# Moving the second stage of batch 1 ahead of the first stage of batch 2 in a woven FFT and expert kernel

## The chip, the cores and the metric

The kernel runs on one core of one Trainium2 chip. The metric is the device time of one execution in microseconds (us). The time before is 1304.29 us, the median of three runs (1298.82 to 1309.32).

## The reference, cut to what matters

```
X = fft(x, axis=1); X = fft(X, axis=2); x = X.real      # 8 batches of 2496 x 256
logits = x @ w_gate                                     # 19968 rows, 8 experts
expert_idx = argmax(logits); gate_w = softmax(logits)[expert_idx]
for e in range(8):                                      # rows sorted by expert
    h = maximum(x_sorted[lo:hi] @ w1[e], 0)             # 256 -> 1024
    y_sorted[lo:hi] = h @ w2[e]                         # 1024 -> 256
out = gate_w * y                                        # in the old order of the rows
```

So each batch is first transformed (a Fourier transform over 2496 places, then one over 256 columns), each of its rows picks one of eight experts, and the rows go through that expert's two matrices.

## The kernel before, in words

The kernel treats the batches one after another and weaves three kinds of work into one order of instructions, written out by Python generators. Every engine then runs its own queue strictly in that order.

**First stage** (`first`, lines 325 to 347). A batch is loaded in three parts (`xq`, line 289, by SP's DMA queue). DVE folds each part (`fold`, lines 295 to 306), TensorE multiplies it by waves (tile `s`), ACT copies the result to `t` (line 321), and a DMA writes it to the scratch `Td` in DRAM (line 342; for batches above 1 it is issued by SP). After the third part `regroup` (line 354) reads `Td` back in another arrangement, as two tiles `t`.

**Second stage** (`second`, lines 361 to 413). For each half of a batch there is a small rotation (tile `pr`), then groups (TensorE `p<-table,t`, ACT copy `zz`, line 379), then five windows: TensorE `p<-table,zz`, ACT `zs` (line 405), DVE `lg` and `rows` (lines 408 and 410). The half ends in `route` (lines 416 to 457): DVE makes the one-hot choice `oh`, TensorE ranks the rows (`rk`), DVE works out the places. The half's ten sets of 128 rows then stand in the list `waiting`. `send` takes one of them, casts its places on ACT (`pi`, line 467) and scatters the rows to the table `Xs` with an indirect DMA of POOL (line 236). Batch 0's casts are not needed.

**Experts** (`experts`, lines 699 to 844). `plan` (lines 476 to 521) works out on DVE, on one partition, which expert and which rows each block of a round has. A block of 256, 128 or 512 rows is fetched from `Xs` by five DMAs of SP (`xb`, lines 532 and 536), with two more for its expert's weights (`w_sb`, lines 542 and 544). DVE and ACT turn the rows (`xT`, lines 580 and 583). TensorE multiplies by the first matrix (`ph`), ACT and DVE apply the relu in turn (`hT`, lines 796 and 794), TensorE multiplies by the second (`py`), ACT scales (`y`, line 835), and POOL scatters the rows to the output. The first round has two blocks of 256 rows and four of 128 from batch 0 alone, the second has blocks of 256 from batch 1.

**The order.** `mixed(b)` says what lies beside the experts: it weaves the first stage of batch b+1 with the second stage of batch b. The main loop takes a unit of expert work and then as many side steps as are due, with a `send` after each (batches under 4). Before the first block can be multiplied, the rows of batch 0 must be in `Xs` and fetched again. In the meantime TensorE has only side work. The fixed number of side steps before the first block is turned is 9 in line 744.

**The end.** `pads` scatters eight sets of padding rows to `Xs` (line 236), one after each of the first eight steps of the last round.

PSUM tiles of the side work share one tag with three buffers, `xq` has three buffers, weights have three.

Of the kernel before, what the change touches and what calls it, by code (L numbers as in the profile page):

```python
# [15 lines left out]
ALU = mybir.AluOpType  # L16
ACTF = mybir.ActivationFunctionType
AX_X = mybir.AxisListType.X
# [17 lines left out]
E, F = 8, 1024  # L36
# [10 lines left out]
def free(ap, offset, *dims):  # L47
    return bass.AP(ap.tensor, ap.offset + offset, [list(ap.ap[0])] + [list(d) for d in dims])


def bc(ap, axis, n):
    shape = list(ap.shape)
    shape.insert(axis, n)
    return ap[tuple([slice(None)] * axis + [None])].to_broadcast(shape)
# [129 lines left out]
LATE = 4  # L184
SHARE, EARLY, ROOM = 0.8, 0.7, 1.2
AHEAD = 12
WARM = 16
MOST = max(k for now in rounds() for _, k, _ in now)

# [26 lines left out]
def kernel(ctx: ExitStack, tc, x, w_gate, w1, w2, out):  # L216
    nc = tc.nc
    vec, act, pool = nc.vector, nc.scalar, nc.gpsimd

    def mm(o, lhsT, rhs, start=True, stop=True, **kw):  # L220
        nc.tensor.matmul(o, lhsT=lhsT, rhs=rhs, start=start, stop=stop, **kw)  # L221
# [47 lines left out]
    con, k = {}, 0  # L269
# [91 lines left out]
    def second(b):  # L361

        t4 = None

        def turn_last(h):

            nonlocal t4
            t4 = ahead.pop((b, "t4", h))
            n = min(HALF, NG - h * HALF)
            pr = pm_.tile([GP, HALF], F32, tag="m", name="pr")  # L370
            mm(pr[:, 0:n], con["rot"][:], t4[0:GP, 0:n, H])
            act.copy(t4[0:GP, 0:n, H], pr[:, 0:n])

        def group(g):
            i, n = g % HALF, LAST if g == NG - 1 else GP
            p2 = pm_.tile([128, 2, n], F32, tag="m", name="p2")
            for c in range(2):
                mm(p2[:, c], t4[0:GP, i, c * H:(c + 1) * H], con["m2"][:, c, 0:n])
            act.copy(zz[:, :, g * GP:g * GP + n], p2[:])  # L379
            if g == HALF - 1:  # L380
                turn_last(1)

        def mirror(rows, k):
            act.copy(free(rows[:], (k + 1) * W + D - 1, [-W, 2], [-1, H - 1]),
                     free(rows[:], k * W + 1, [W, 2], [1, H - 1]))

        turn_last(0)
        yield
        group(0)
        yield  # L390
        group(1)
        yield
        for h in range(2):
            rows = sp.tile([128, NSL, W], F32, tag="rows", name="rows")
            lg = sp.tile([128, NSL, E], F32, tag="lg", name="lg")
            for i in range(HW):
                w, k = HW * h + i, 2 * i
                if w + 2 < NG:
                    group(w + 2)
                p3 = pm_.tile([128, 2 * NY + 2 * E + 1], F32, tag="m", name="p3")  # L400
                z = zz[:, :, 128 * w:128 * (w + 1)]
                mm(p3[:, 0:NY + 2 * E], z[:, 0], con["rd"][:, 0, 0:NY + 2 * E], True, False, skip_group_check=True)
                mm(p3[:, NY:], z[:, 1], con["rd"][:, 1], False, True, skip_group_check=True)
                zs = sp.tile([128, NY + 1], F32, tag="zs", name="zs")
                act.copy(zs[:], p3[:, NY + 2 * E:])  # L405
                if i:
                    mirror(rows, k - 2)
                vec.tensor_copy(lg[:, k:k + 2], p3[:, NY:NY + 2 * E].rearrange("p (m e) -> p m e", m=2))  # L408
                for m, op in enumerate((ALU.add, ALU.subtract)):
                    vec.scalar_tensor_tensor(rows[:, k + m, 0:NY], p3[:, 0:NY], zs[:, 0:1], zs[:, 1:],  # L410
                                             op0=ALU.add, op1=op)
                yield
            mirror(rows, k)
            yield from route(b, h, rows, lg)
# [58 lines left out]
    bk = {n: bt[:, lo:hi] for n, (lo, hi) in where.items()}  # L473
    gone = bk["cap"]

    def plan(b, size, k, last):

        nonlocal gone

        def one(name, *dims, dt=F32):  # L480
            return cp.tile([1, *dims], dt, tag="p_" + name, name="p_" + name, bufs=2)

        nb, ni = one("nb", E), one("ni", E, dt=I32)
        ce, ex, rb, n = one("ce", E), one("ex", E), one("rb", E), one("n", E)
        lo = one("lo", E, E)
        vec.tensor_tensor(nb[:], base[0:1], gone[:], op=ALU.subtract)
        vec.tensor_scalar(ni[:], nb[:], size - 1.0 if last else 0.0, None, op0=ALU.add)
        vec.tensor_scalar(ni[:], ni[:], size.bit_length() - 1, None, op0=ALU.logical_shift_right)
        vec.tensor_copy(nb[:], ni[:])
        vec.tensor_tensor(lo[:], bk["low"].rearrange("p (a b) -> p a b", a=E), bc(nb[:], 1, E), op=ALU.mult)  # L490
        vec.reduce_sum(ce[:], lo[:], axis=AX_X)
        vec.tensor_tensor(ex[:], ce[:], nb[:], op=ALU.subtract)
        yield
        vec.scalar_tensor_tensor(rb[:], ex[:], -float(size), gone[:], op0=ALU.mult, op1=ALU.add)
        ge, ei = one("ge", MOST, E), one("ei", MOST)
        val, eq, rw = one("val", MOST, E + 1), one("eq", MOST, E + 1), one("rw", MOST)
        vec.tensor_tensor(ge[:], bc(bk["i"], 2, E), bc(ce[:], 1, MOST), op=ALU.is_ge)
        vec.reduce_sum(ei[:], ge[:], axis=AX_X)
        yield
        vec.tensor_tensor(eq[:], bc(ei[:], 2, E + 1), bc(bk["e9"], 1, MOST), op=ALU.is_equal)  # L500
        vec.memset(val[:, :, E:E + 1], float(E * CAP))
        vec.scalar_tensor_tensor(val[:, :, 0:E], bc(bk["i"], 2, E), float(size), bc(rb[:], 1, MOST),
                                 op0=ALU.mult, op1=ALU.add)
        yield
        vec.tensor_tensor(val[:], val[:], eq[:], op=ALU.mult)
        vec.reduce_sum(rw[:], val[:], axis=AX_X)
        tab = cp.tile([1, 2, MOST], I32, tag="p_tab", name="p_tab", bufs=4)
        vec.tensor_copy(tab[:, 0], rw[:])
        vec.tensor_scalar(tab[:, 1], ei[:], E - 1.0, None, op0=ALU.min)
        if last:  # L510
            cnt = cp.tile([1, 1], I32, name="cnt")
            vec.tensor_copy(cnt[:], ce[:, E - 1:E])
            tabs["cnt"] = cnt
        if not last:

            vec.tensor_scalar(n[:], ex[:], -1.0, float(k), op0=ALU.mult, op1=ALU.add)
            vec.scalar_tensor_tensor(n[:], n[:], 0.0, nb[:], op0=ALU.max, op1=ALU.min)
            nxt = one("gone", E)
            vec.scalar_tensor_tensor(nxt[:], n[:], float(size), gone[:], op0=ALU.mult, op1=ALU.add)
            gone = nxt  # L520
        yield
        tabs[b, size, last] = tab
# [68 lines left out]
    def below(w, eng):  # L591

        ws2 = sp.tile([128, 3, FC // 2, H], F32, tag="t4", name="ws2")
        return right(ws2, *(w[:, 4 * f:4 * f + 4, k * H:(k + 1) * H] for f in (1, 0) for k in range(2)), eng=eng)
# [104 lines left out]
    def experts(todo):  # L699
# [4 lines left out]
        xbs, got, xT, used, left, rest = [], [], None, None, None, None  # L704
# [30 lines left out]
        for k, (b, size, last, at) in enumerate(todo):  # L735
            n, m = size // 128, BIG // size
            if not k:
                while todo[0][:3] not in tabs:
                    yield 0, False
                fetch_some(0, 1)  # L740
                while b not in whole:
                    yield 0, True
                fetch_some(0)
                for _ in range(9):
                    yield 0, False
                for xT in turn(b, size, xbs[0][0]):
                    pass
# [53 lines left out]
            if follow:  # L801
# [9 lines left out]
                if follow[1] == BIG and quartered(*follow[:2]):  # L811
                    rest = below(got[0][1], pool)
# [30 lines left out]
            if follow and follow[1] == BLK and quartered(*follow[:2]):  # L843
                rest = below(got[0][1], vec)
# [29 lines left out]
    def ahead_of(b):  # L874

        yield from first(b)
        regroup(b, 0)
        regroup(b, 1)

    def mixed(b):  # L880

        one, two = (ahead_of(b + 1) if b + 1 < B else iter(())), second(b)
        for _ in range(3):
            next(one, None)
            yield
        for k, _ in enumerate(two):
            if k % 2:
                next(one, None)
            yield
        yield from woven(close(b), one)  # L890
        yield from through(b)
# [9 lines left out]
    nc.sync.dma_start(out=wg[:], in_=w_gate)  # L901
    for k in range(WARM):
        pw = pse.tile([128, D], F32, tag="bd"[k % 2], name="py")
# [35 lines left out]
    work = experts(todo)  # L939
    steps = {b: mixed(b) for b in range(1, B)}  # L940
    for b in range(1, B):

        done, due, room = 0, 0.0, 0.0
        side = chain(steps[b], islice(steps.get(b + 1, iter(())), AHEAD))
        ticks = TICKS + AHEAD * (b == 1)
        if b == 1:
# [23 lines left out]
        for _ in side:  # L970
            send()
    rest = pads(B - 1)
    for _ in work:
        next(rest, None)


_INS = ["x", "moe_w_gate", "moe_w1", "moe_w2"]
# [46 lines left out]
```

## Time and profile before

| what | value |
|---|---|
| median of three runs | 1304.29 us (1298.82 to 1309.32) |
| profiled execution, its own time | 1306.36 us |
| its span | 1304.6 us |
| mean granted TensorE clock | 0.970 |
| TensorE busy | 1227.3 us, 94% of the span |
| DVE, ACT, POOL busy | 54%, 33%, 28% |
| DMA | 249.71 MB, mean 191 GB/s |

The profile's second part cuts the span into 40 slices of 32.6 us and gives each engine's busy share in tenths. TensorE is at nine or more nearly everywhere except in the first eight slices. The chain that ended last is 86% TensorE. So what an edit is worth is what it takes from, or adds to, the time in which TensorE stands still.

### The profile page before, as it was taken

Reading aid. Unit: us, or ns where it says so; the run is one execution under the profiler, and the core shown is the slowest. Engines: PE = TensorE matmul, PEld = TensorE weight load, DVE = VectorE, ACT = ScalarE, POOL = GpSimd, SP = SyncE. Lnnn points to the kernel's source line nnn. Section 1 sums busy time; section 2 is a strip of 40 time slices with the busy share of each in tenths; the row PEclk is TensorE's granted clock in tenths of the full one; section 3 lists DMA queues with packets and bytes.
Section 4 is the critical chain, followed back from the end, with each engine's and each line's share of the span. In section 5 each row is a group of like instructions: output and inputs, shape, how many; then the busy total and the mean of one; then the engine's idle time right before and its main releaser. Section 6 shows DMA issues by size and latency. Waiting matters only on the chain.

```text
span 1304.6 us, 21062 instructions
## 1 busy us (share of the span) xinstructions
PE 1227.3 (94%) x6905; PEld 1080.0 (83%) x6905; DVE 700.7 (54%) x1772; ACT 436.0 (33%) x1096; POOL 361.8 (28%) x355
## 2 busy tenths in 40 slices
PE   5668898999999999999999999999999999999996
PEld 3557797876788888888888888888889999999995
DVE  4455433433456555566546455675468774444662
ACT  1423222332334343434334343432233332222232
POOL 0245215125014311351114411351354221111112
PEclk8869898999999999999999999999999999999998
DMA  8859697657446445483335535453444238787786
GB/s 244 264 182 326 211 339 262 180 188 237 136 133 216 160 146 158 145 264 108 112 115 182 159 104 161 126 164 105 120 131 163 90 106 295 275 277 270 282 285 236
DMA packets 163210, 249.71 MB, mean 191 GB/s; under 512 B 118601, under 2 KB 130227, under 8 KB 143516
## 3 DMA queue, kind: packets, MB, share of 16 engines
q1 hardware_dynamic: 146327, 203.28, 49.0%
q0 software_dynamic: 15888, 42.14, 9.0%
q10 hardware_dynamic: 885, 2.94, 0.7%
q8 instruction: 56, 0.92, 0.3%
q14 instruction: 54, 0.44, 0.1%
HBM read 194.91 MB, written 54.83 MB: 191 GB/s over the span
## 4 chain that ended last, share of the span: by engine, by line
PE 86%; DVE 4%; DMA 4%; another core or an unknown queue 2%; issue 2%; ACT 1%; SPq 1%; POOL 0%; POOLq 0%; DVEq 0%; ACTq 0%
PE py L221 32%; PE ph L221 10%; PE c L221 10%; PE a L221 9%; PE p L221 6%; PE d L221 6%; PE b L221 5%; PE e L221 4%; PE s L221 3%; DMA w_sb<-in_moe_w_dram 2%; DMA xq<-in_x_dram 1%; DMA Td<-t 1%; SPq L532 1%; PE rk L221 0%
## 5 line engine op out<-in xcount | busy, mean ns | idle before, releaser
L221 PE MATMUL py<-w_sb,hT 128*128 128x256 f32 x2016 | 457.8, 381 | 8.3 <-DVE hT L794 8.3
L221 PEld LDWEIGHTS py<-w_sb,hT 128*128 128x128 f32 x2016 | 379.8, 191 | 59.1 <-DVE hT L794 8.7
L236 POOL DMA_INDIRECT out_dram<-y,ro x163 | 162.8, 999 | 735.8 <-ACT y L835 494.3
L236 POOL DMA_INDIRECT Xs<-rows,pi x160 | 163.5, 1022 | 199.0 <-ACT pi L467 81.6
L221 PE MATMUL ph<-xT,w_sb 128*128 128x128 f32 (+2 forms) x992 | 173.5, 330 | 9.0 <-DVE hT L794 5.3
L221 PEld LDWEIGHTS ph<-xT,w_sb 128*128 128x128 f32 x992 | 137.0, 194 | 34.3 <-issue 18.6
L835 ACT ACTIVATE y<-py,xb 128x256 f32<-128x256 f32 x129 | 61.1, 474 | 244.4 <-PE py L221 206.2
L221 PE MATMUL a<-xT,w_sb 128*128 128x256 f32 (+1 forms) x512 | 118.2, 358 | 2.1 <-ACT hT L629 1.3
L794 DVE TENSOR_SCALAR hT<-ph 128x512 f32<-128x512 f32 x43 | 29.7, 691 | 144.3 <-issue 73.6
L619 DVE TENSOR_TENSOR u<-p,b 128x512 f32<-128x512 f32 x57 | 39.2, 687 | 125.1 <-PE b L221 90.3
L221 PEld LDWEIGHTS a<-xT,w_sb 128*128 128x128 f32 x512 | 89.0, 190 | 14.7 <-ACT hT L629 2.5
L408 DVE COPY lg<-p 128x16 f32<-128x16 f32 x80 | 13.9, 174 | 142.4 <-ACT zs L405 131.8
L629 ACT ACTIVATE hT<-a 128x512 f32<-128x512 f32 x57 | 34.0, 597 | 157.7 <-PE a L221 116.7
L583 ACT ACTIVATE xT<-xT 128x256 f32<-128x256 f32 (+1 forms) x94 | 36.4, 387 | 135.3 <-DVE xT L580 88.6
L221 PE MATMUL s<-xq,w 104*112 104x256 f32 (+2 forms) x208 | 60.4, 413 | 13.1 <-DVE xq L297 12.6
L221 PEld LDWEIGHTS p<-table,t 120*128 120x128 f32 x352 | 55.3, 206 | 17.1 <-issue 6.3
L221 PE MATMUL c<-xT,ws 128*128 128x256 f32 (+1 forms) x256 | 60.5, 364 | 6.9 <-DVE hT L625 6.7
L221 PE MATMUL p<-table,t 120*128 120x120 f32 (+1 forms) x352 | 58.2, 292 | 8.3 <-ACT zz L379 3.4
L221 PE MATMUL p<-table,zz 128*128 128x145 f32 (+1 forms) x320 | 57.6, 305 | 7.8 <-issue 4.8
L580 DVE STREAM_TRANSPOSE xT<-xb 128x512 f32<-128x512 f32 (+1 forms) x94 | 58.1, 625 | 4.7 <-DMA xb<-Xs 4.7
L796 ACT ACTIVATE hT<-ph 128x512 f32<-128x512 f32 x55 | 32.8, 597 | 80.2 <-PE ph L221 59.1
L221 PE MATMUL b<-xs,ws 128*128 128x256 f32 (+1 forms) x256 | 58.7, 356 | 0.0
(145 smaller groups left out, 1739.8 us busy)
## 6 DMA issues: line engine op xcount, KB each, us to landing
w_sb<-in_moe_w_dram SPq DMA_DIRECT2D x132, 1024.0 KB
xq<-in_x_dram SPq DMA_DIRECT2D x24, 896.0 KB
xb<-Xs SPq DMA_DIRECT2D x112, 128.0 KB
Td<-t SPq DMA_DIRECT2D x18, 448.0 KB
t<-Td SPq DMA_DIRECT2D x8, 768.0 KB
t<-Td SPq DMA_DIRECT2D x8, 640.0 KB
xb<-Xs SPq DMA_DIRECT2D x52, 64.0 KB
xb<-Xs SPq DMA_DIRECT2D x100, 32.0 KB
```

The costliest lines, as they stand in the source:

```text
L221: nc.tensor.matmul(o, lhsT=lhsT, rhs=rhs, start=start, stop=stop, **kw)
L236: return unordered(pool.indirect_dma_start(out=dst, out_offset=bass.IndirectOffsetOnAxis(ap=idx, axis=0), in_=rows, in_offset=None, bounds ...
L408: vec.tensor_copy(lg[:, k:k + 2], p3[:, NY:NY + 2 * E].rearrange("p (m e) -> p m e", m=2))
L532: taken(nc.sync.dma_start(out=flat[32 * q:32 * q + 32, 0:2 * size].rearrange("p (j e) -> p j e", e=64), in_=Xs[ds(row, size), 64 * q:64 * ...
L580: vec.transpose(free(xT[:], 256 * h, [32, n // 32], [BIG, 2], [1, 32]), free(xb, 512 * h, [64, n // 32], [1, 2], [2, 32]))
L583: act.activation(odd, odd, ACTF.Copy, scale=-1.0)
L619: vec.tensor_tensor(u2[:], p1[:], b[:], op=add)
L629: act.activation(h11, a[:], ACTF.Relu)
L794: vec.tensor_scalar(o, ph[:], 0.0, None, op0=ALU.max)
L796: act.activation(o, ph[:], ACTF.Relu)
L835: act.activation(y[:], py[:], ACTF.Copy, scale=meta[:, i, 1:2])
```

## The change

The second stage of batch 1 is taken up to its eleventh step before the first stage of batch 2 is begun; eleven steps are the five windows of the first half and its route as far as the ranks (`rk`); the places are worked out in the step after. The steps before the first block is turned become 12. `plan` works on as many entries of its small tables as the round has blocks, and no longer on the largest number, 21. The padding rows at the end are written after every fourth step of the last round.

```diff
+FRONT = 11
...
-        ge, ei = one("ge", MOST, E), one("ei", MOST)
-        val, eq, rw = one("val", MOST, E + 1), one("eq", MOST, E + 1), one("rw", MOST)
-        vec.tensor_tensor(ge[:], bc(bk["i"], 2, E), bc(ce[:], 1, MOST), op=ALU.is_ge)
-        vec.reduce_sum(ei[:], ge[:], axis=AX_X)
+        ge, val, eq = (one(name, MOST, E + 1)[:, 0:k] for name in ("ge", "val", "eq"))
+        ei, rw = (one(name, MOST)[:, 0:k] for name in ("ei", "rw"))
+        count = bk["i"][:, 0:k]
+        vec.tensor_tensor(ge[:, :, 0:E], bc(count, 2, E), bc(ce[:], 1, k), op=ALU.is_ge)
+        vec.reduce_sum(ei, ge[:, :, 0:E], axis=AX_X)
         yield
-        vec.tensor_tensor(eq[:], bc(ei[:], 2, E + 1), bc(bk["e9"], 1, MOST), op=ALU.is_equal)
+        vec.tensor_tensor(eq, bc(ei, 2, E + 1), bc(bk["e9"], 1, k), op=ALU.is_equal)
         vec.memset(val[:, :, E:E + 1], float(E * CAP))
-        vec.scalar_tensor_tensor(val[:, :, 0:E], bc(bk["i"], 2, E), float(size), bc(rb[:], 1, MOST),
+        vec.scalar_tensor_tensor(val[:, :, 0:E], bc(count, 2, E), float(size), bc(rb[:], 1, k),
                                  op0=ALU.mult, op1=ALU.add)
         yield
-        vec.tensor_tensor(val[:], val[:], eq[:], op=ALU.mult)
-        vec.reduce_sum(rw[:], val[:], axis=AX_X)
+        vec.tensor_tensor(val, val, eq, op=ALU.mult)
+        vec.reduce_sum(rw, val, axis=AX_X)
         tab = cp.tile([1, 2, MOST], I32, tag="p_tab", name="p_tab", bufs=4)
-        vec.tensor_copy(tab[:, 0], rw[:])
-        vec.tensor_scalar(tab[:, 1], ei[:], E - 1.0, None, op0=ALU.min)
+        vec.tensor_copy(tab[:, 0, 0:k], rw)
+        vec.tensor_scalar(tab[:, 1, 0:k], ei, E - 1.0, None, op0=ALU.min)
...
-                for _ in range(9):
+                for _ in range(12):
                     yield 0, False
                 for xT in turn(b, size, xbs[0][0]):
                     pass
...
         one, two = (ahead_of(b + 1) if b + 1 < B else iter(())), second(b)
+        if b == 1:
+            yield from islice(two, FRONT)
         for _ in range(3):
             next(one, None)
             yield
...
     rest = pads(B - 1)
-    for _ in work:
-        next(rest, None)
+    for k, _ in enumerate(work):
+        if k % 4 == 0:
+            next(rest, None)
```

## The prediction

> **What bounds the kernel now.** I read the 40 slices first, then TensorE's idle stretches, then the timelines of POOL and SP in those stretches. The slices show where TensorE is not full and where its granted clock falls:
>
> ```profile
> PE   5668898999999999999999999999999999999996
> PEclk8869898999999999999999999999999999999998
> ```
>
> Each slice is 32.6 us. TensorE misses time in the first six or seven and in the last. All the gaps together are 71 us, and the change touches those from 60 to 140 us (first block of batch 0 awaited, then its last products) and those at the padding rows at the end. TensorE's waits between 60 and 180 us (line, releaser, total, count, longest):
>
> ```profile
> PE py L221 <- DVE hT L794: 8.3, 1, 8.3
> PE p L221 <- issue: 7.5, 2, 4.8
> ```
>
> and TensorE's timeline where they lie:
>
> ```profile
> 91.37 2.01 PE L221 MATMUL ph<-xT,w_sb 128*128 128x256 f32 x8 [1.76 <-DVE ro L753]
> ...
> 136.25 6.59 PE L221 MATMUL py<-w_sb,hT 128*128 128x256 f32 x20 [8.29 <-DVE hT L794]
> 142.68 0.28 PE L221 MATMUL pr<-t,table 120*120 120x6 f32 x2
> ```
>
> The twenty py after the gap take 6.59 us. Sixteen in another place (105.11 to 108.56) took 3.45, so twenty are 4.3 and the halved clock after the gap costs 2.3. The awaited hT is one operation of DVE, idle before it for 12.19 us with a releaser that the profile calls "remote". SP's timeline says when it came free:
>
> ```profile
> 122.56 6.46 SPq L532 DMA_DIRECT2D xb<-Xs  x4
> 131.17 0.73 SPq L536 DMA_DIRECT2D xb<-Xs  x1
> 135.46 0.71 SPq L542 DMA_DIRECT2D w_sb<-in_moe_w_dram  x1
> 136.26 0.33 SPq L544 DMA_DIRECT2D w_sb<-in_moe_w_dram  x1
> 143.38 1.89 SPq L532 DMA_DIRECT2D xb<-Xs  x4
> ...
> 206.08 5.25 SPq L532 DMA_DIRECT2D xb<-Xs  x4
> 213.54 0.34 SPq L544 DMA_DIRECT2D w_sb<-in_moe_w_dram  x1
> ```
>
> The same seven DMAs of a block took 14.0 us from 122.56, 7.8 from 206.08, and 4.4 from 143.38. The two slow ones fall into back-to-back rows of POOL's placements: 118.81 to 133.87 (twelve, one each 1.28 us) and 204.02 to 211.40. SP was through 2.7 and 2.5 us after the row's end. TensorE stood still there too, 10.2 us at 121 to 136 and 5.3 at 208 to 214. So I read a row of placements as what holds the hand-offs between other engines. This is inferred from three coincidences; two other rows (306 to 317, 420 to 430) stop TensorE nowhere.
>
> **The change, part by part.**
>
> *Up to the first block.* Four s (1.9 us) leave the stretch 60 to 91, two windows (groups and products) and the first rank come in (1.9 + 0.4): TensorE has idle time there, so this costs nothing by itself. POOL is the slow queue:
>
> ```profile
> 65.75 0.97 POOL L236 DMA_INDIRECT Xs<-rows,pi  x1 [0.30 <-issue]
> 67.03 1.77 POOL L236 DMA_INDIRECT Xs<-rows,pi  x1 [0.30 <-issue]
> 69.11 1.57 POOL L236 DMA_INDIRECT Xs<-rows,pi  x1 [0.30 <-issue]
> ...
> 74.82 1.59 POOL L236 DMA_INDIRECT Xs<-rows,pi  x1 [0.30 <-issue]
> ...
> 80.56 1.47 POOL L236 DMA_INDIRECT Xs<-rows,pi  x1 [0.30 <-issue]
> ```
>
> Four placements are 2.5 us longer than 0.97 in sum, each while DVE folds batch 2 (the first under the 1.21 us at 66.75). The folds now come later, so the row ends at 79.5 and no longer at 82.03. But DVE now has, ahead of the rows' transposition, five windows' lg and rows, the whole choice of expert and one fold. Second window: its products start 0.8 after the row's end, as now (82.03 to 82.83), and lg follows 1.5 to 1.7 later: 81.8. Three more windows at 1.1 each (lg at 54.94 to 58.06) or 1.95 (82.83 to 84.80): I take 1.5, 86.3. Then 0.7 for rows, 2.7 for the choice (49.64 to 52.36), 2.7 for the fold (1.21 + 0.66 + 0.67 + 0.16), 0.76 from transposition to ph: **first ph at 93.1**, 1.7 later than 91.37. Bounds: 90.3, if the row holds no window (1.1 apart from 78.99) and only the choice, fold and landing count; 97 with 1.95 a window and the row not shortened.
>
> *From first ph to the second rank of batch 1.* It is 24.4 us now (91.37 to 115.74). Eight py pairs (3.45), seven s (2.17), the first rank (0.33), one window (0.94) and small gaps (0.2) leave: 17.3. Call its end T.
>
> *From T to the rotation `pr` of batch 2.* The queue in between: rank 0.3, s 0.9, py 3.45, s 0.9, ph 1.73, s 0.9, ph 1.73, s 1.6, ph 3.45, py 3.45, so 18.4 us with nothing awaited; the last s ends at T + 11.5. The gaps of 1.9 and 8.3 and the slow 2.3 go if placements come earlier: the first ten do (they need only the first rank, now done before the first ph), the second ten still form one row, from T + 3.1 (115.74 to 118.81 now) for 12.8 us to T + 15.9.
>
> This adds a wait. `pr` needs `t` of batch 2, which needs its last Td, and on SP both now stand **behind the seven DMAs of the third 128 block** (before, Td, xq and t went ahead of it). SP gets to these at about T + 9.2, inside the row, is through by 2.6 after the row's end, T + 18.5; then Td, 5.9 to issue t (113.76 to 119.69 now), 4.9 until usable, as for batch 0 (t issued 29.11, pr at 33.97 after "1.16 <-DMA t<-Td"): T + 29.3, a wait of **10.9 us** for the 18.4 of cover. Behind `pr` on TensorE wait the groups, the last products of block 1 and the 128 blocks; POOL's outputs wait for those. Bounds: SP at its normal 4.4 and t 3.45 after Td (291.61 to 295.06) give T + 21.9, a wait of 3.5; SP at 14.0 gives T + 34, a wait of 15.5.
>
> *From `pr` to 179.65*, where both orders meet again: 36.97 now, plus 3.45 for half of block 1's second products, which now come behind `pr`: 40.4. The halved clock after the wait: 2.3 as above (0 to 2.3). So 93.1 + 17.3 + 18.4 + 10.9 + 40.4 + 2.3 = 182.4 against 179.65: **+2.8 us** (bounds 169.9 and 190.9, so -9.8 to +11.3).
>
> *The padding rows.* Eight in a row at 943.6 to 954:
>
> ```profile
> 951.67 1.13 PE L221 MATMUL a<-xT,w_sb 128*128 128x256 f32 x4 [0.64 <-issue]
> 956.06 2.03 PE L221 MATMUL c<-xT,ws 128*128 128x256 f32 x4 [2.39 <-DVE hT L625]
> 957.88 2.75 PE L221 MATMUL a<-w_sb,hT 128*128 128x128 f32 x16
> ```
>
> Gaps 0.64 and 2.39; c takes 2.03 for 1.03 at 950.00, and a 2.75 for 1.95: 4.8 together. Spread over the round, one, three or four at a time, they hold POOL for 5.1 us at most (four by 1.28), and the gaps begin only 7 us into the present row: **-4.5** (bounds -4.8, and +1 if a placement now disturbs another step).
>
> The Trainium skill, "SBUF — State Buffer", section "SBUF: two separate sides", says that only DVE and GpSimd share a port pair and TensorE waits on neither; by it no row of placements could hold TensorE directly, the pads' gain would be 0 and the sum 1307.0. The trace's 2.39 us of TensorE awaiting hT speaks for an indirect hold, through DVE. "TensorE: Matmul & The Clock Gate", section "What's actually happening", has the clock halve after an idle window of about 3.4 us; the trace has it halved behind a gap of 2.39. By that rule 1.8 of the pads' 4.8 would not come back, and the sum would be 1304.3.
>
> *Plans.* Six operations of DVE go from some 0.33 to 0.16 to 0.20, 0.9 us a plan; DVE is busy for 54% and TensorE waits for a plan nowhere in the trace: 0 (down to -1 if the last places reach SP sooner). After 179.65 the order is the old one; shifts of later placement rows against SP: 0, within 3.
>
> **Sum.** 2.8 - 4.5 = -1.8 (rounded) on the profiled execution's own 1306.36 (span 1304.6), 2.07 over the median of 1304.29; against the median 1304.29 - 1.8 = **1302.5**. Own range 1295 to 1309.
>
> **Rivals.**
>
> R1, the row no longer holds anything that is near its due time: first ph 90.3, wait 3.5, no halved clock, pads -4.8, plans -1. 169.9 - 179.65 = -9.8; with the rest -15.6: **1288.7**. For it: two rows hold TensorE nowhere, and ten of the twenty placements come earlier. Against it: ten remain in one row, and SP's DMAs stand in it.
>
> R2, the third 128 block's fetch takes SP's slow pace, so `t` is usable at T + 34: a wait of 15.5, 4.6 more than forecast: **1307.1**, slower than before; with the first ph at 97 too, 1311.0. It decides once `t` is usable later than about T + 31, where the forecast's gain is used up. For it: the one trace of this very situation (122.56) had 14.0. Against: in that case SP began early in the row, here late.
>
> R3, spreading the pads brings nothing, since four in a row still meet a step that needs DVE: -1.8 + 4.5 = +2.7, **1307.0**. Against: the gaps' place, late in the row.
>
> **How the numbers follow.** Forecast 0.48, R1 0.24, R2 0.18, R3 0.10. A measurement here tells about 1% (13.0 us) from no change: below 1291.2 lies most of R1 (0.17) and a tail of the forecast in which later rows also gain (0.05), so faster 0.22; above 1317.3 lies R2 with its late first block and lost pads, or later rows gone worse: 0.13; the same 0.65. The range, 1288 to 1314, takes in R1's and R2's values and leaves out some 0.2.
>
> **What would show it.** Right: first ph between 92 and 95; POOL's batch 0 row over by 80, with no placement above 1.1; no gap of 8 us at py; instead a wait of 8 to 13 us at `pr` for DMA t<-Td, with SP's fetch of the third 128 block just before its Td; no gap above 1 us near the end at a or c. Wrong: `pr` without a wait (R1), a wait above 15 (R2), the gap of 2.4 still before c (R3), or a new gap behind 180 us, where I expect none.

## The result, and the profile after

The changed kernel takes 1312.58 us (median of 8 runs, 1307.84 to 1317.68) against 1303.72 us (8 runs): the ratio is 1.0069, 95% interval 1.0046 to 1.0093. It is slower, by 8.9 us in the medians; 1302.5 was forecast. The profiled execution has a span of 1310.2 us for 1304.6, and the waits of TensorE that the profile lists sum to 78.7 us for 70.0.

The slices of its page; PE's third digit (65 to 98 us) has fallen from 6 to 3, its fifth (131 to 164) from 8 to 5:

```profile
PE   5639598999999999999999999999999999999996
PEclk9969799999999999999999999999999999999998
```

TensorE's waits between 60 and 195 us (line, releaser, total, count, longest):

```profile
PE p L222 <- ACT zz L380: 14.5, 3, 8.6
PE py L222 <- DVE hT L796: 8.5, 2, 7.5
PE pr L222 <- DMA t<-Td: 7.5, 2, 5.6
```

The wait of py for hT is still there (7.5 for 8.3), a wait of `pr` has joined it, and p waits 10 us longer for `zz` than before (14.5 for 4.4); part of that is only another name, since the waits of p for which the profile finds no releaser ("issue") fell from 7.5 to 2.0. TensorE's timeline:

```profile
82.53 1.34 PE L222 MATMUL p<-table,zz 128*128 128x145 f32 x4 [8.62 <-ACT zz L380]
...
98.05 5.63 PE L222 MATMUL ph<-xT,w_sb 128*128 128x256 f32 x16 [3.81 <-DVE ro L755]
...
142.23 2.07 PE L222 MATMUL py<-w_sb,hT 128*128 128x256 f32 x4 [7.45 <-DVE hT L796]
149.87 0.56 PE L222 MATMUL pr<-t,table 120*120 120x6 f32 x2 [5.57 <-DMA t<-Td]
...
152.12 5.82 PE L222 MATMUL py<-w_sb,hT 128*128 128x256 f32 x16
```

The first ph starts at 98.05 (91.37 before). The products at which both orders meet again start at 194.81 for 179.65: **15.2 us are lost there**. From there on it gains: 12.7 late at the last step ahead of the old pads' gaps (c, 962.74 for 950.00), 7.6 behind them (b, 968.04 for 960.47), 6.7 at TensorE's end. Of the first 2.5 us most come between 205 and 240 us; no run takes them apart.

Where the first 6.7 us go is seen on ACT and DVE. ACT, which copies `zz` for the windows:

```profile
82.11 0.62 ACT L380 COPY zz<-p 128x240 f32<-128x240 f32 x2 [9.47 <-remote]
```

The products that it copies had been ready since 73.9. POOL's row of batch 0 ended at 79.07, its last lines being evenly 0.97:

```profile
66.61 0.97 POOL L237 DMA_INDIRECT Xs<-rows,pi  x1 [0.30 <-issue]
...
78.10 0.97 POOL L237 DMA_INDIRECT Xs<-rows,pi  x1 [0.30 <-issue]
```

So the row is 2.5 us shorter, as forecast, but this hand-off from TensorE to ACT came only 3 us after its end. All five windows came behind it, and then on DVE the fold and the transposition:

```profile
94.81 1.16 DVE L307 TENSOR_TENSOR xq<-xq 104x1024 f32<-104x1024 f32 x1
...
97.28 0.70 DVE L582 STREAM_TRANSPOSE xT<-xb 128x512 f32<-128x512 f32 x1
```

SP's timeline shows the wait of `pr`:

```profile
126.28 2.81 SPq L534 DMA_DIRECT2D xb<-Xs  x4
...
132.17 0.32 SPq L546 DMA_DIRECT2D w_sb<-in_moe_w_dram  x1
133.57 0.01 SPq L343 DMA_DIRECT2D Td<-t  x1
135.74 0.35 SPq L290 DMA_DIRECT2D xq<-in_x_dram  x1
144.63 0.98 SPq L355 DMA_DIRECT2D t<-Td  x2
```

Batch 2's last Td stands behind the third 128 block's fetch, as forecast; but then t is issued 11.1 us after Td, where 5.9 was reckoned. POOL's row beside it has not become shorter but longer:

```profile
118.32 0.97 POOL L237 DMA_INDIRECT out_dram<-y,ro  x1 [1.73 <-ACT pi L468]
119.60 1.46 POOL L237 DMA_INDIRECT Xs<-rows,pi  x1 [0.30 <-ACT pi L468]
...
139.06 0.97 POOL L237 DMA_INDIRECT Xs<-rows,pi  x1 [0.31 <-issue]
```

It is sixteen indirect DMAs (fourteen placements and two outputs) up to 140.03, for thirteen, counted in the same way, up to 133.87 before; the awaited hT came 1.5 us after its end (DVE at 141.49).

At the pads nothing stands still and the clock stays full:

```profile
962.74 1.03 PE L222 MATMUL c<-xs,ws 128*128 128x256 f32 x4
963.60 1.03 PE L222 MATMUL a<-xT,w_sb 128*128 128x256 f32 x4
...
965.33 1.09 PE L222 MATMUL c<-xT,ws 128*128 128x256 f32 x4
966.26 1.95 PE L222 MATMUL a<-w_sb,hT 128*128 128x128 f32 x16
968.04 1.95 PE L222 MATMUL b<-ws,hT 128*128 128x128 f32 x16
```

In the trace of before the same c and b stand at

```profile
950.00 1.03 PE L221 MATMUL c<-xs,ws 128*128 128x256 f32 x4
...
960.47 1.95 PE L221 MATMUL b<-ws,hT 128*128 128x128 f32 x16
```

### The profile page after: what moved, and what is told of

Its sections match the earlier page's. It is cut to its first block, busy times and chain, and to the rows that moved or that the text cites. A ratio compares the mean times of both kernels' runs of the same rounds, so it can differ in the third digit from the quotient of the medians.

```text
span 1310.2 us, 21057 instructions
## 1 busy us (share of the span) xinstructions
PE 1225.4 (94%) x6905; PEld 1079.9 (82%) x6905; DVE 689.9 (53%) x1772; ACT 436.4 (33%) x1096; POOL 360.9 (28%) x355
## 5 line engine op out<-in xcount | busy, mean ns | idle before, releaser
L237 POOL DMA_INDIRECT Xs<-rows,pi x160 | 163.0, 1018 | 205.5 <-ACT pi L468 63.6
L222 PE MATMUL d<-xT,w_sb 128*128 128x256 f32 (+1 forms) x256 | 58.7, 356 | 0.0
```

What stands on the lines that cost most here:

```text
L237: return unordered(pool.indirect_dma_start(out=dst, out_offset=bass.IndirectOffsetOnAxis(ap=idx, axis=0), in_=rows, in_offset=None, bounds ...
```

## The experiments

The experiments ran in five sets, each with its own runs of the kernel before. With the first comparison there are six, and they fall into two kinds: in three the kernel before has a median of 1303.7, 1297.5 and 1303.4 us, in three one of 1276.7, 1276.9 and 1276.9. The traces show where they differ. In the slower kind TensorE stops when POOL works through a row of indirect DMAs ("a set that holds", the hold being the delay of hand-offs between the other engines); in the other it doesn't, for the same kernel and the same row. TensorE's listed waits sum to 70.0 and 63.6 us in the two traces of the kernel before where rows hold. Where they don't, there is no trace of that very kernel, but its nearest relatives (`pads_only`, `row_out`, `row_out_2`) have 46.7 to 48.7. The sets that hold are the first comparison, that of `before_again`, `after_again`, `t_first` and `row_real`, and that of `t_clear` and `old_paced_3`. Ratios are taken within a set only.

**Which part loses.** `pads_only` is the kernel before with

```diff
-    for _ in work:
-        next(rest, None)
+    for k, _ in enumerate(work):
+        if k % 4 == 0:
+            next(rest, None)
```

> The old order and the old plans, with the padding rows spread, nothing else. Theory (a row of POOL's indirect DMAs holds the hand-offs between the other engines, and the pads' row is one): the gaps of 0.64 and 2.39 us before a and c and the halved clock behind them go, 4 to 5 us less than the kernel before. Rival (the gaps there have another cause, or return in the next row): within 1.5 us of it.

Measured, in a set that doesn't hold: 1275.95 against 1276.65 us, ratio 0.9994 (0.9981 to 1.0007). No gain; its trace has no gap at the pads, but neither has that of `row_plain` (the old pads, same kind of set) one over 1.2 us there. The expectation was for a set that holds, where the changed kernel's trace gained 5.2 us at that place.

`old_order` is the changed kernel without the early second stage:

```diff
-        if b == 1:
-            yield from islice(two, FRONT)
...
-                for _ in range(12):
+                for _ in range(9):
```

> The changed kernel with the old order of batches 1 and 2 (and the old nine steps); short plans and spread pads stay. Theory: the order alone made the kernel slower, and this one is as fast as with the spread pads alone, 4 to 5 us less than before, some 13 us less than the changed kernel. Rival (the short plans cost or gain something by themselves): more than 2 us away from the kernel with the spread pads alone.

Measured in the same set: 1273.7 us, 0.9983 (0.9966 to 1.0000). That is 2.3 us under `pads_only`, just over the 2 us that the expectation gave to its rival; but the two intervals overlap, so a small gain of the short plans can't be told from none. The short plans and the pads cost nothing measurable and may gain 0.2%. So what the changed kernel loses, the order loses.

`after_again` and `after_third` are the changed kernel, unchanged, in a set of each kind.

> The changed kernel, unchanged, on the same chip. Theory (its loss is the wait of pr for t of batch 2, since Td and t stand behind the third 128 block's fetch): without holds the first ph at 88 to 90 us, a wait of 12 to 15 us at pr, and 1.2% to 1.4% slower than before. Rival (the loss is the later first ph, which folds ahead of the transposition make): a wait at pr under 5 us.

> The changed kernel once more, on a chip that may or may not hold. Theory (the wait at pr is the order's own and does not need a hold): on a chip that doesn't hold, first ph at 88 to 90 us, a wait of 12 to 15 us at pr, 1.2% to 1.4% slower than before; on one that holds, as before: first ph at 98, gaps at py and pr of 13 us together, 0.7% to 1.0% slower. Rival: without a hold no loss.

Measured: 1310.0 against 1297.5 us where rows hold, 1.0102 (1.0069 to 1.0135), and 1291.93 against 1276.92 where they don't, 1.0122 (1.0092 to 1.0152). The loss needs no hold. Without one, the first ph comes at 86.83 and the gap at py is gone, but that at `pr` is larger. TensorE in `after_third`:

```profile
86.83 5.13 PE L222 MATMUL ph<-xT,w_sb 128*128 128x256 f32 x16 [7.02 <-DVE ro L755]
...
138.40 0.57 PE L222 MATMUL pr<-t,table 120*120 120x6 f32 x2 [14.47 <-DMA t<-Td]
```

and SP there:

```profile
119.05 0.36 SPq L544 DMA_DIRECT2D w_sb<-in_moe_w_dram  x1
119.60 0.33 SPq L546 DMA_DIRECT2D w_sb<-in_moe_w_dram  x1
121.05 0.34 SPq L343 DMA_DIRECT2D Td<-t  x1
123.47 0.35 SPq L290 DMA_DIRECT2D xq<-in_x_dram  x1
132.21 0.98 SPq L355 DMA_DIRECT2D t<-Td  x2
```

SP issues the seven DMAs of the fetch in 5.4 us here (114.55 to 119.93), and the row holds nobody; still Td, issued right behind two weights of 1024 KB each, lets t go only 11.2 us later.

`before_again` is the kernel before, for its trace.

> The kernel before, unchanged, for a trace beside the others on this chip. Theory (where the rows of POOL's indirect DMAs hold no hand-offs, as in the traces of the last four kernels, the kernel before is itself some 27 us faster): either the first ph at about 86 us, no gap of 8 us at py and none at the pads, and some 1277 us; or, where they hold, the trace of before again, with 1304 us.

Measured: 1298.27 us (one run), with the gaps of before (5.9 us at py, 3.8 near 210, 3.1 at the pads).

**The late first ph.** `turn_early` has 10 for the 12 steps, so that the fold stands behind the transposition. `fold_early` puts the fold into POOL's row:

```diff
         if b == 1:
+            next(one)
+            next(one)
             yield from islice(two, FRONT)
-        for _ in range(3):
-            next(one, None)
+        for k in range(3):
+            if b != 1 or k == 2:
+                next(one, None)
             yield
```

> The changed kernel with 10 steps in the place of 12 before the first block is turned: the fold of batch 2's first part then stands behind the transposition on DVE. Theory (DVE's own queue is 2.6 of the lateness of the first ph): the first ph at 95.4 us and no longer at 98.05, and the end some 2.5 us less than in the changed kernel. Rival (the lateness is only passed on to the wait of pr): first ph earlier, end unchanged within 1 us.

> The changed kernel with the fold of batch 2's first part (both steps) ahead of batch 1's second stage, that is inside POOL's row of batch 0, where the kernel before had it. Theory (while DVE folds, POOL's placements take longer and hand-offs between the other engines get through, so the folds helped): ACT's zz that came at 82.11 in the changed kernel comes at 68 to 77, at least two windows are done before the row ends, and the first ph is at 91 to 93. Rival (the fold only stood in front of the transposition): zz still after 81, first ph at 95.4.

Both came in a set that doesn't hold, so they can't tell whether folds open the hold. They measured 1292.81 (1.0118, 1.0094 to 1.0142) and 1291.04 us (1.0115, 1.0093 to 1.0136), with the first ph 6.4 and 7.4 us after the row's end, as `after_third` (6.4) and `old_order` (6.3). There neither the fold nor the windows set the first ph: it follows the row. Both have the wait at `pr`, 14.5 and 13.7 us, and both cost as much as `after_third` in its set (1.0122). The changed kernel itself has no run in their set, so what the place of the fold is worth is open.

**The wait at pr.** `t_first` (set that holds) and `t_first_2` (set that doesn't) are the changed kernel with one fetch of SP moved; the queues of the other engines are as they were:

```diff
-    ahead = {}
+    ahead, stored = {}, []
...
                 n = len(xbs)
+                if k + len(got) >= 3 and not stored:
+                    break
...
         regroup(b, 1)
+        if b == 2:
+            stored.append(b)
```

> The changed kernel with one edit: the fetch of the third 128 block (five DMAs of its rows, two of its weights) is issued by SP behind batch 2's last Td and both t, and no longer ahead of its Td. Every other engine's order is the same. Theory (the fetch is the cause): Td lands 5 us after its issue and no longer 11, the wait at pr falls from 12 to 15 us to 0 to 4 us, and the kernel is some 11 us faster than the changed one. Rival (t waits for the products s, which come too late in any case): the wait at pr falls by 3 us at most.

> The changed kernel with the third 128 block's fetch behind both t of batch 2, and nothing else. Theory: on a chip that doesn't hold the wait at pr is 2 to 5 us (no hold between Td's landing and t), and the block's own rows come late at its ph by 2 to 6 us, so it wins 6 to 10 us of the 12 to 17 that the order costs. On a chip that holds: 8 us less than the changed kernel again. Rival: the wait only moves to the block's ph and nothing is won.

Measured: 1301.67 us, 8.3 less than the changed kernel of its set (1.0045, 1.0024 to 1.0066, against before), and 1284.75 us, 7.2 less (1.0060, 1.0038 to 1.0081). The wait at `pr` is 7.95 us in the one and, in `t_first_2`,

```profile
130.08 0.56 PE L222 MATMUL pr<-t,table 120*120 120x6 f32 x2 [7.93 <-DMA t<-Td]
```

with SP:

```profile
115.89 0.31 SPq L343 DMA_DIRECT2D Td<-t  x1
116.31 0.39 SPq L290 DMA_DIRECT2D xq<-in_x_dram  x1
122.44 1.01 SPq L355 DMA_DIRECT2D t<-Td  x2
```

The fetch is half of it, in two ways: against `after_third`, Td is issued 1.0 us after the last s begins and no longer 4.4, and from Td to t it is 6.6 us and no longer 11.2. The forecasts of a wait of 0 to 4 and of 2 to 5 us were too good, for a wait of 8 stays; the gain of 7.2 us is as forecast, and no new wait at the block's ph takes its place in `t_first_2`, so the rival is refuted. `t_clear` is `t_first` without what else SP has issued about Td, two loads of 896 KB for batch 3 (one ahead of Td, one right behind it):

```diff
-                if b:
+                if b and (b != 2 or q == 1):
                     load(b + 1, q - 1)
...
             stored.append(b)
+            load(3, 1)
+            load(3, 2)
```

> The changed kernel with the third 128 block's fetch behind both t of batch 2, and the loads of batch 3's second and third part behind them too, so that batch 2's last Td and t have the queue's DMAs to themselves. Theory (what is left of the wait at pr, 7.9 us, is partly Td and t sharing the DMA engines with loads issued just before them): Td lands 3 us after its issue (5.5 now), t 5 us after (7.5 now), the wait at pr falls to 2 to 4 us, and the kernel comes within 0.4% of before. Rival (the wait is only the chain's own length): the wait stays over 6 us.

Measured, in a set that holds: 1304.22 against 1303.36 us, 1.0011 (0.9992 to 1.0030). Its TensorE:

```profile
138.17 0.56 PE L222 MATMUL pr<-t,table 120*120 120x6 f32 x2 [2.34 <-DMA t<-Td]
```

and SP (the second of the two Td is the last one, issued at 128.27):

```profile
122.64 5.94 SPq L343 DMA_DIRECT2D Td<-t  x2
131.84 0.98 SPq L355 DMA_DIRECT2D t<-Td  x2
132.93 1.37 SPq L290 DMA_DIRECT2D xq<-in_x_dram  x2
```

Td to t is 3.6 us, 7.0 in `t_first` (129.28 to 136.25); rows hold in both. So the wait came of what SP issued beside Td and t; whether it delayed them by its place in the queue or by the DMA engines that it shares with them, these runs don't part. The kernel is level with the one before, but that doesn't clear the order: the spread pads are in it too, and they gained 5.2 us in the changed kernel's trace. Between 60 and 240 us TensorE is idle for 38.7 us in `t_clear`, 45.4 in the changed kernel and 33.9 in the one before (29.1 in `before_again`), and the first ph is still late (97.3).

**What a row of placements holds.** `row_real` is the kernel before with twelve more indirect DMAs behind the 24th output (POOL is idle there), into a table `Dm` that nobody reads:

```diff
+        ins = placed(dst, idx, rows, last, group)
+        if group == "out":
+            trial[0] += 1
+            if trial[0] == AT:
+                for j in range(12):
+                    placed(Dm, di[:, j:j + 1], pad[:], 12 * 128 - 1, "dm")
+        return ins
...
```

> The kernel before with twelve more indirect DMAs of POOL in a row, each writing 128 rows of zeros to a table of its own that nobody reads, at about 332 us, where POOL is idle for 23 us. Theory (a row holds hand-offs on some chips): on a chip that holds, ACT and DVE stand still for 5 us or more from the fourth of the row on and TensorE has a gap of 3 us or more near 340 us; on a chip that doesn't, no gap over 0.5 us. Rival (the holds come of the SP traffic beside the rows): no gap on either.

Measured, in a set that holds: one run of 1305.02 us beside 1297.5. The row lies at 327.5 to 342.8. TensorE, which in the kernel before has no gap there:

```profile
335.44 0.77 PE L222 MATMUL p<-table,zz 128*128 128x145 f32 x4 [0.81 <-issue]
...
341.42 0.48 PE L222 MATMUL p<-table,t 120*128 120x120 f32 x2 [2.85 <-ACT t L384]
...
345.41 1.98 PE L222 MATMUL ph<-xT,w_sb 128*128 128x512 f32 x4 [1.28 <-ACT hT L808]
348.49 1.98 PE L222 MATMUL ph<-xT,w_sb 128*128 128x512 f32 x4 [1.10 <-DVE hT L806]
```

Together 6.0 us, from the sixth of the row on. A row by itself, sharing neither tile nor table with the waiting work, makes TensorE stand still, in one run of a set that holds. The forecast inferred this from coincidences; here it is shown. All three long waits are for ACT or DVE, so the hold is of the hand-offs and not of TensorE itself.

`row_out` and `row_out_2` have indices beyond the table (nothing is written), `row_plain` 24 plain fills of a tile (0.53 us each) in its place.

> As the run with twelve more indirect DMAs in a row at 332 us, but with every index beyond the table, so that nothing is written: POOL's instructions stay, the data doesn't move. Theory A (POOL's making of the row holds the hand-offs): on a chip that holds, TensorE's gaps between 330 and 350 us again sum to 4 to 8 us (6.0 with the writes). Theory B (the DMA traffic of the row holds them): under 1 us. Whether this chip holds is seen in the same trace at the rows near 130 us.

> The kernel before with twelve more indirect DMAs in a row at 332 us whose indices all lie beyond the table, so that nothing is written. On a chip that holds (seen at the rows near 130 us of the same trace): theory A (POOL's making of the row holds the hand-offs) has TensorE's gaps between 330 and 350 us at 4 to 8 us in sum, theory B (the row's data traffic does) under 1 us. On a chip that doesn't hold it says nothing.

> As the two runs with a row at 332 us, but with 24 plain fills of a tile by POOL in the place of the indirect DMAs. Theory (only indirect DMAs hold, whose descriptors POOL makes; a busy POOL doesn't): TensorE's gaps between 330 and 350 us under 0.5 us in sum. Rival (any busy POOL holds hand-offs): 3 us or more.

All three came in sets that don't hold: 1275.74, 1273.6 and 1280.9 us (one run each), no gap over 0.6 us at their place. They decide nothing. Whether POOL's making of the row, its data, or any long work of POOL holds the others stays open.

**Breaking up the rows.** `old_paced`, `old_paced_2` and `old_paced_3` are one kernel: `old_order` with

```diff
+    calls = 0
...
+        nonlocal calls
+
+        calls += 1
-        if waiting:
+        if waiting and (waiting[0][0] not in (1, 2) or len(waiting) > 10 or calls % 2 == 0):
```

> The old order with short plans and spread pads, and the placements of batches 1 and 2 sent at every second step only, so that their rows break up (after the first 20 at most nine in a row, before twelve and seventeen). Theory (rows hold): on a chip that holds, the gap at py near 130 us falls below 3 us and those near 210 and 228 below 2 us each, 8 to 14 us less than before with the pads' part. On a chip that doesn't hold: within 3 us of before. Rival (slower sending makes a block late): a new wait for xb after 200 us.

> The old order with short plans, spread pads and the placements of batches 1 and 2 at every second step. Theory: on a chip that holds, the gap at py near 130 us falls below 3 us, those near 210 and 228 below 2 us each, and it is 10 to 16 us faster than before; on one that doesn't, 7 us again. Rival (rows of nine hold as well as rows of twelve): the gaps at py and at 210 stay within 2 us of before.

> The old order with short plans, spread pads and paced placements, for a chip that holds, if this is one. There: the gap at py near 130 us below 3 us, those near 210 and 228 below 2 us each, 10 to 16 us faster than before. Rival (rows of nine hold as well as rows of twelve): the gaps stay within 2 us of before. On a chip that doesn't hold: 7 to 10 us faster again.

Measured: 1269.47 us, 0.9935 (0.9921 to 0.9949), and 1267.07 us, 0.9927 (0.9904 to 0.9950), without a hold; 1296.59 us, 0.9944 (0.9921 to 0.9966), with one. It is **faster than the kernel before in each of its three sets**, and by 24.9 us than the changed kernel (`after_third`) in the one set that has both. Where rows hold, TensorE's gaps between 120 and 160 us are

```profile
128.52 2.08 PE L222 MATMUL py<-w_sb,hT 128*128 128x256 f32 x4 [2.31 <-issue]
133.01 7.31 PE L222 MATMUL py<-w_sb,hT 128*128 128x256 f32 x20 [2.42 <-DVE hT L800]
149.10 3.52 PE L222 MATMUL py<-w_sb,hT 128*128 128x256 f32 x8 [3.48 <-DVE hT L800]
158.00 0.48 PE L222 MATMUL p<-table,t 120*128 120x120 f32 x2 [1.38 <-ACT t L373]
```

9.6 us in all (10.2 in the trace of before, 7.7 in `before_again`), and 2.2 for 7.3 in the stretch of 205 to 235. The gap at py is under 3 us as forecast, but it has only been cut into several, the one of 3.5 being new; so shorter rows still hold, and the gain is 6.8 us where 10 to 16 was expected. Without a hold "within 3 us of before" was expected at first, and it is 7.4 and 9.9 us. Part of this is a wait of `pr` of batch 3 for t near 210: 4.2 and 2.9 us in the relatives of the kernel before from the same two sets (`row_out`, `row_out_2`), none in `old_paced` and `old_paced_2`. The rest is not traced.

`new_paced` is the changed order with the edits of `fold_early`, `t_first` and `old_paced`.

> The changed order with three edits: the fold of batch 2's first part ahead of batch 1's second stage, the third 128 block's fetch behind both t of batch 2, and the placements of batches 1 and 2 at every second step. Theory (these are the three causes of the loss): first ph at 91 to 93 us on a chip that holds and 86 on one that doesn't, a wait at pr of 2 to 5 us (15 us from the last s to pr fall to 10 to 12 without a hold), no gap over 3 us at 200 to 250; 4 to 10 us less than before on a chip that holds. Rival (the wait at pr is the order's own): 6 us or more there, and no faster than before.

Measured, without a hold: 1277.97 against 1276.86 us, 1.0014 (0.9999 to 1.0029). The wait at `pr` is gone and a new one stands in its place, at the 128 block whose fetch was put off:

```profile
140.26 3.75 PE L222 MATMUL ph<-xT,w_sb 128*128 128x128 f32 x16 [5.32 <-DVE xq L298]
```

DVE had waited 5.2 us for `xb` before it. The order brings t and this block's fetch to SP at one time, and one of them is late. `old_paced`, in the same set, is 8.5 us faster. The rival's "no faster than before" is right, though not by the wait that it named; the forecast for a set that holds has no run.

## Why the prediction was wrong

The forecast put the two orders' meeting point at 182.4 us and it is 194.8, beyond even its upper bound of 190.9. Two steps of it failed: the first window was placed inside POOL's row, and Td's landing behind the fetch was priced too low. The 12.4 us between are these terms.

| term | forecast | trace | off by |
|---|---|---|---|
| first ph | 93.1 | 98.05 | +5.0 |
| first ph to the second rank | 17.3 | 19.3 (to 117.37) | +2.0 |
| second rank to `pr`, waits in it | 29.3 | 32.5 (to 149.87) | +3.2 |
| `pr` to the meeting point | 42.7 | 44.9 | +2.2 |

**First ph: the first step that failed, and the term furthest off.** The forecast took the first window as done at 78.99 within POOL's row, and had four windows behind it from 81.8. In the trace the first window itself comes at 82.53; lg then comes at 84.25, 86.50, 87.91, 89.96 and 91.60, and the last is 5.3 us later than the 86.3 reckoned. The choice (2.7), the fold (2.5) and the 0.77 behind them were right. The shorter row was credited as a gain. In the sets that hold, the first window comes at 69.7 to 75.4 us in the four traces of the old order, where the row takes 26.4 to 27.9 us, and at 77.8 to 82.6 in the four of the new order, where it takes 25.4. That the folds, by slowing the row, let hand-offs through fits this, but the kernel made for it ran where nothing is held; so it is argued and not shown. This term weighs most in the forecast's sum, but not in the loss: without a hold the first ph is no later than in the old order (86.83, against 86.73 in `pads_only`), and the changed kernel loses 1.2% all the same. Of these 15.0 us `t_first_2` wins back 7.2 by moving the fetch alone, and a wait of 7.9 at `pr` is left beside the 7.8 us still lost.

**From ph to the rank.** Halved clock, for which the forecast had no term: the first sixteen ph take 5.5 us after a gap of 3.81 and the 3.25 before the rank (granted clock 0.50 from 96 to 102 us); sixteen take 3.5 elsewhere.

**Wait at pr: the second step that failed.** Right in its place, wrong in its price. Last s to Td took 5.0 us and not 7.0; t to `pr` 5.2 for 4.9; Td to t 11.1 for 5.9. That last price was read from a Td with no fetch right ahead of it. The forecast moved Td behind the weights and counted the time of *issuing* them; the time of *moving* their 2048 KB, before Td's own 448, it put at nothing. `after_third` shows the same 11.2 without any hold, and `t_first` (7.0 and 6.6) and `t_clear` (3.6) take it away in two steps. R2 had the right size for a set that doesn't hold (15.5; 14.5 measured), by the wrong cause: it made SP slow.

The 7.5 us at py were expected to be gone, since the first ten placements were to come ahead of the row. Only six did; four joined it, and the row ended 22.7 us after the second rank and not 15.9. The 7.5 us are part of the same 14 us in which t is awaited (`after_third` has them all at `pr`), so they add little.

**After pr.** The 2.3 for the halved clock was right (5.82 for 3.5); 1.0 at an hT comes on top, and some 1.2 in `pr` and the groups ahead of these products, at the same clock (0.50 from 150 to 156 us).

**Pads and plans.** 5.2 us measured for 4.5 in a trace that holds; nothing in a set that doesn't. Plans: nothing that can be told from noise. The prediction set an indirect hold against the Trainium skill, "SBUF — State Buffer", section "SBUF: two separate sides", by which TensorE and ScalarE never wait on another engine at their ports. `row_real` bears the indirect hold out for TensorE; but two of its waits there are for ScalarE (2.85 and 1.28 us), so the hold doesn't go through DVE alone, as the prediction had it, and what delays ScalarE no run shows. R3 fails in the first comparison.

**The chances.** "Slower by over 1%" had 0.13; the median says 0.7% and the repeats 1.0 and 1.2%. The median lies inside the range of 1288 to 1314, but by luck: the meeting point was missed by more than its bounds allow, and gains behind it (2.5 us ahead of the pads, for which the forecast had 0, and 5.2 at them) made up for part of it. R1 came true in one thing where rows don't hold (first ph at 86.8), and even there the kernel is slower, since the wait at `pr` doesn't depend on it.

## What to carry to other kernels

When a step is moved behind a fetch in a DMA queue, add the fetch's bytes, not only its issue times, to the landing of everything behind it; a small store that a later load waits for goes ahead of a large prefetch. A unit of work taken earlier pulls another one later: name what the other one feeds, here t, and how much cover is left between its last product and its first use (7 us for a chain of 21 to 22, and of 15 and 11 in the two runs with less beside it). Before a gap is put down to the order of the work, see whether the same kernel has it in another set of runs.

## What was not expected of the hardware

In some sets of runs a row of POOL's indirect DMAs (0.97 us each, 0.30 between) holds hand-offs among the other engines, up to 3 us beyond its end, and in others the same row holds nothing; the kernel before takes some 1300 or 1277 us accordingly, 2%. Each of the five sets of experiments ran on a chip of its own; whether the difference belongs to the chip or to a condition of it, no run here tells. And TensorE's clock was halved behind gaps of 2 to 4 us in many places: the sixteen ph after a gap of 2.16 us in `old_paced_3` took 5.41 us, at a granted clock of 0.58 and 0.57. But not behind all: in `before_again` the c after a gap of 3.08 us took 1.13 us for 1.03, at 1.00.
